# Pairs of neighbouring PSUM banks, the diagonal on GpSimd, and the last rows fetched by index, in a fused RWKV-6 and mixture-of-depths kernel

## The chip, the cores and the metric

The kernel runs on one core of a Trainium2 chip. A core has five engines that run side by side, each with its own queue of instructions, worked off in order: TensorE (PE; its weight loads are shown as PEld), VectorE (DVE), ScalarE (ACT), GpSimd (POOL) and SyncE (SP), which here issues most transfers. They wait for one another by semaphores. Data lies in SBUF, 128 rows of it, and matmuls write to PSUM, which has eight banks of 512 fp32 values a row. The metric is the device time of one execution, in microseconds (us).

## The reference, cut to what matters

```python
# attention: batch 4, heads 8, sequence 768, head size 48
for t in range(S):
    cur = np.einsum('bhd,bhe->bhde', u[None] * kt, vt)
    y[:, :, t] = np.einsum('bhd,bhde->bhe', rt, state + cur)
    state = wt[:, :, :, None] * state + np.einsum('bhd,bhe->bhde', kt, vt)
x = y.transpose(0, 2, 1, 3).reshape(B, S, H * D)          # 4 x 768 x 384

# mixture of depths: 128 of the 768 rows of each batch go through an expert
scores = np.einsum('bsd,d->bs', x, w_gate)
out = x.copy()
for b in range(B):
    top_idx = np.argpartition(-scores[b], capacity)[:capacity]
    xe = x[b, top_idx]
    ye = np.maximum(xe @ w1, 0.0) @ w2                    # 384 -> 1024 -> 384
    g = 1.0 / (1.0 + np.exp(-scores[b, top_idx]))
    out[b, top_idx] = x[b, top_idx] + g[:, None] * ye
```

A state that decays with w runs along the sequence. The term with u is each time step's own contribution: r times u times k, summed over the head's 48 values, times v of the same step. That number per head and time step is what the kernel calls "own", and it stands on the diagonal of the matrix of scores.

## The kernel before, in words

The sequence of each batch is cut into steps of 256 time steps (two chunks of 128), and the eight heads into two groups of four. A unit n is one step of one group of one batch: 4 batches x 3 steps x 2 groups = 24 units. `attention(P, n)` lists the work of a unit:

- SP loads w, k, r and v (line 257). The tiles have six buffers each, so a load waits until the unit six earlier is done with its buffer.
- POOL multiplies neighbouring rows of w (`w01`, L423), ACT takes the logarithm (`ln`, L427), PE sums it along the time with a triangular matrix (`U`, L432), DVE adds (`three`, L436), and ACT takes three exponentials of the result (`K1`, `K0`, `R`, L440 to L447). PE and ACT make the decay of a chunk (`D`, L457; `dec`, L462), and ACT applies it to the carried state (`begin`, L471).
- DVE scales k and r with the exponentials (`kr`, L479). PE transposes the result in two parts (`tr0`, `tr1`, L511), and ACT copies them out of PSUM (`cp0`, `cp1`, L520, tile krt).
- For the diagonal, POOL multiplies r by k and by u (`rk`, L488, and `ru`, L490), DVE sums over the head (`own`, L493), and ACT writes each sum on a diagonal of the score tile `sc` (`diag`, L501): eight small activations, `diag` (a 0/1 pattern of 128x64) times one number a row.
- PE makes the chunk's contribution to the state (`kv`, L537), DVE decays and adds it (`mid`, L549 and L554; `end`, L562).
- PE makes the scores (`S`, L609) and the first half of the product with the carried state (`rs1`, L578). DVE copies the scores that lie before the diagonal over the tile `sc` with a mask (`choose`, L626). PE then multiplies by v (`av`, L594) and adds the rest of the product with the state (L578 again).
- ACT copies the output out of PSUM (`x`, L641). DVE sums it with the gate's weights (`gate`, L649). After the second group of a step SP stores the rows (L664), and `compare` begins the ranking: PE spreads the scores (`ev`, L674), ACT copies them (`every`, L677), DVE counts which are larger (`cmp`, L680).

After six units a batch is complete and `mixture(P, b)` lists the rest. PE and DVE finish the rank (`columns`, L698; `rank`, L707), DVE marks for each of 128 places the row that has it (`pick`, L710), PE turns that into row numbers (`chosen`, L716; `idx`, L722). POOL fetches the rows from the output in HBM by index (`fetch`, L732), PE transposes them (`xt`, L744), ACT copies (`xec`, L754), and PE runs the two products of the expert (`p0` to `p7`, L788; `s0` to `s7`, L800) with ACT's relu in between (L794). DVE joins gate, product and row (`ye`, L805), and POOL scatters the rows back (`put`, L808). For the last batch (`held`) the rows' transpose is not taken from the fetched rows: PE gathers it from the rows of x that still lie in SBUF, by 18 fp32 products with `pick` (L747). There `pick` and the row numbers are fp32; elsewhere they are bf16. The fetch is made there too, for the gate and the sum at the end.

What sets the order is a written table. `Plan.add` only lists an operation with its engine, a planned duration, what it reads and writes, and which PSUM banks it opens or closes. Each operation gets a place `n + PHASE[name]` (for `mixture` n is the unit after the batch), and each engine does its operations in order of these places. The numbers only order the operations of one engine. `Plan.order` goes through the engines' queues with the planned durations, to settle the order of the program and which bank each PSUM tile gets. All PSUM is one tile, `psum`, of eight banks. `kv`, `S` and the output `Y` open two banks each, all other PSUM work one. Before the change any two free banks, those free for longest, made a pair (a, z), seen as `psum[:, a:z + 1:z - a, :]`. Operations marked `lock` are those of POOL and DVE that the planner keeps from running at the same time. SP, POOL's transfers and the waits follow from the same lists: an operation waits for those it depends on, and everything behind it in its engine's queue waits with it.

Of the kernel before, what the change touches and what calls it, by code (L numbers as in the profile page):

```python
# [18 lines left out]
L = 128  # L19
# [9 lines left out]
    "mid": -3.387, "cross": -3.695, "end": -3.208, "S": -2.042, "rs1": -2.003, "choose": -3.097,  # L29
# [3 lines left out]
    "won": 0.735, "columns": 2.189, "rank": 1.054, "pick": 1.358, "chosen": 3.464, "idx": 2.603,  # L33
    "fetch": 4.846, "rows": -40.331, "xt": 5.06, "xec": 6.795, "gates": 5.066, "gexp": 8.198,
# [3 lines left out]
    "s7": 14.354, "gate": -2.165, "krk": -0.95, "krr": -0.9, "c_table": -27.848,  # L38
    "c_strict": -29.361, "c_ident": -30.222, "c_iota": -32.474, "c_sums0": -28.494,
    "c_kr0": -65.518, "c_mask": -38.859, "c_sc0": -6.477, "c_sums1": -20.14, "c_kr1": -14.021,  # L40
    "c_sc1": -7.253, "c_sums2": -7.757, "c_kr2": -5.147, "c_sc2": -34.768, "c_ones": -41.327,
    "c_front": 0.4, "c_count": -37.113, "c_slots": -25.476,
# [13 lines left out]
class Plan:  # L56
# [37 lines left out]

    def order(self, banks):
# [15 lines left out]
        while len(out) < len(ops):  # L111
            best = None
            for e in line:
                if head[e] == len(line[e]):
                    continue
                n = line[e][head[e]]
                o = ops[n]
                count = sum(c for _, c in o["opens"])
                if any(seen[d] is None for d in o["deps"]) or count > len(free):
                    continue  # L120
                s = clock[e]
                if e == "PE" and o["tiles"] != tiles:
                    s += self.TURN[o["tiles"]]
                for d in o["deps"]:
                    s = max(s, ends[d] + self.AGAIN[e] if ops[d]["eng"] == e else seen[d])
                asked = s
                if o["lock"]:
                    s = max(s, port)
                if count:
                    s = max(s, sorted(free.values())[count - 1])  # L130
                if (best is None or s < best[0] - 1e-9 or s < best[0] + 1e-9 and o["lock"]
                        and ops[best[1]]["lock"] and asked < best[2]):
                    best = (s, n, asked)
            assert best is not None, "the order cannot be kept"
            s, n, _ = best
            o = ops[n]
            e = o["eng"]
            if e == "PE":
                tiles = o["tiles"]
            for name, c in o["opens"]:  # L140
                got = sorted(free, key=lambda i: (free[i], i))[:c]
                place[name] = tuple(sorted(got))
                for i in got:
                    free.pop(i)
            ends[n] = clock[e] = s + o["dur"]
            seen[n] = ends[n] + self.DELAY[e]
# [32 lines left out]
def kernel(  # L179
# [49 lines left out]
    def view(where):  # L229
        if len(where) == 1:  # L230
            return psum[:, where[0], :]
        a, z = where
        return psum[:, a:z + 1:z - a, :]
# [16 lines left out]
    xs = several(NT // 2, [L, 2, C], "x")  # L250
# [32 lines left out]
    pick32 = consts.tile([L, NT, L], FP32, name="pick32")  # L283
    ids32 = consts.tile([L, B, NT, 2], FP32, name="ids32")
# [19 lines left out]
    def constants(P):  # L304
# [81 lines left out]
        def _(_):  # L386
# [7 lines left out]
            nc.vector.tensor_copy(out=ids32, in_=ids)  # L394


    def attention(P, n):
# [7 lines left out]
        x = xs[step]  # L405
# [5 lines left out]
        X = f"x{step}"  # L411
# [61 lines left out]
        if not first:  # L473
            P.add("ACT", 0.22, lambda _: decayed(0, before, 0),
# [23 lines left out]
        def diagonal(_):  # L498
            for j in range(J):
                for i in (0, 1):  # L500
                    nc.scalar.mul(  # L501
                        ct[:, j % 2, j // 2, i, i, :], diag, ot[:, j % 2, j // 2, i:i + 1]
                    )
        P.add("ACT", 0.95, diagonal, reads=[OW, "mask"], writes=[SC], at=n, cls="diag")


# [180 lines left out]
    def mixture(P, b, held=False):  # L687

# [3 lines left out]

        pk, numbers = (pick32, ids32) if held else (pick, ids)

        def columns(ps):
# [15 lines left out]
            out=pk, in0=_free(slots, [0, NT], [1, L]), in1=rank.to_broadcast([L, NT, L]),  # L711
            op=ALU.is_equal), reads=["rank", "slots"], writes=["pick"], at=at, cls="pick", lock=True)

        def chosen(ps):
            for c in range(NT):
                nc.tensor.matmul(  # L716
                    ps[:, 0:2], pk[:, c, :], numbers[:, b, c, :],
                    start=(c == 0), stop=(c == NT - 1),
                )
        P.add("PE", 0.7 if held else 0.2, chosen, reads=["pick", "ids"], writes=[ID], at=at, cls="chosen",  # L720
# [19 lines left out]
        def turned(ps):  # L740
            for dc in range(NDC):
                at_dc = slice(dc * L, (dc + 1) * L)
                if not held:
                    nc.tensor.transpose(ps[:, at_dc], xe[z][:, at_dc], ident)  # L744
                    continue
                for c in range(NT):
                    nc.tensor.matmul(  # L747
                        ps[:, at_dc], xs[c // 2][:, c % 2, at_dc], pk[:, c, :],
                        start=(c == 0), stop=(c == NT - 1),
                    )  # L750
        P.add("PE", 2.1 if held else 0.35, turned, reads=["pick"] + [
            f"x{c}{g}" for c in range(NT // 2) for g in (0, 1)] if held else [f"xe{z}"], writes=[XT], at=at, cls="xt", opens=[(XT, 1)],
# [81 lines left out]
    for n in range(N):  # L834
        attention(P, n)
        if n % NU == NU - 1:
            mixture(P, n // NU, held=n == N - 1)
# [88 lines left out]
```

## Time and profile before

| | |
|---|---|
| median of the runs | 236.13 us (231.27 to 239.29, three runs) |
| the profiled execution | 236.0 us, of which the span from first to last instruction is 234.3 |
| mean granted TensorE clock in it | 0.943 |
| busy PE, PEld, DVE, ACT, POOL | 186.0, 158.9, 140.5, 143.2, 87.3 us |
| transfers | 29.44 MB, most of it in packets under 512 bytes |

Rows of instruction groups give a line, an engine, an operation, the tile written and the tiles read, sizes and a count; then the busy time and the mean duration of one in ns; then the idle time of the engine just before them and what ended it. Rows in order of time give the start, the duration, the instruction, and in brackets the idle time before it. Rows of waits give who waited for whom: us in total, times, longest. An fp32 matmul of the expert shows as two records. Matmuls overlap, and their ends are modelled, so PE's busy time is no measure of its best use.

### The profile page before, as it was taken

The numbers are of one execution on the slowest core, as the hardware profiler recorded it, in microseconds if no ns is written. First come the engines' busy times: TensorE is split into PE (matmuls) and PEld (weight loads), VectorE is DVE, ScalarE is ACT, GpSimd is POOL, SyncE is SP. The second block draws the span as 40 slices with busy tenths as digits, with TensorE's granted clock in tenths as the row PEclk, the third lists the DMA queues.
The fourth block names the chain that finished last, engine by engine and source line by source line (L and its number), as shares of the span: only waits on it lengthen the run. The fifth ranks groups of instructions, "written<-read, shape, count | busy, mean of one in ns | idle before, by whom it ended". The sixth has DMA issues, their size and how long they took to land.

```text
span 234.3 us, 10156 instructions
## 1 busy us (share of the span) xinstructions
PE 186.0 (79%) x4313; PEld 158.9 (68%) x4313; DVE 140.5 (60%) x400; ACT 143.2 (61%) x529; POOL 87.3 (37%) x99
## 2 busy tenths in 40 slices
PE   1868977696887697667787979796977999999960
PEld 0657766695777596665786966585966786979830
DVE  7747778687787858656768575659475346410110
ACT  3889889798998768688378475576365342110200
POOL 8876664355355554535315414307000110110110
PEclk9999999999999979799799799999799899999995
DMA  6999999897986948776244013202002103020101
GB/s 159 277 230 272 222 262 255 230 235 178 291 210 151 277 113 250 169 182 165 65 104 105 7 34 86 53 3 70 3 3 69 38 6 99 3 67 0 35 1 48
DMA packets 56853, 29.44 MB, mean 126 GB/s; under 512 B 51296, under 2 KB 55648, under 8 KB 56800
## 3 DMA queue, kind: packets, MB, share of 16 engines
q1 hardware_dynamic: 56288, 27.14, 44.7%
q0 software_dynamic: 512, 1.57, 2.4%
q8 instruction: 36, 0.59, 1.1%
q14 instruction: 17, 0.14, 0.2%
HBM read 23.20 MB, written 5.51 MB: 123 GB/s over the span
## 4 chain that ended last, share of the span: by engine, by line
PE 55%; ACT 16%; DVE 16%; issue 6%; POOL 2%; DMA 2%; SPq 0%; POOLq 0%; DVEq 0%; ACTq 0%
ACT sc L501 12%; PE psum L788 10%; PE psum L594 10%; DVE sc L626 9%; PE psum L511 9%; PE psum L800 8%; PE psum L537 3%; PE psum L609 3%; PE psum L578 3%; PE psum L432 3%; DMA u_bc<-in_u_dram 2%; ACT x L641 2%; PE psum L747 2%; PE psum L674 1%; DVE kr L479 1%
## 5 line engine op out<-in xcount | busy, mean ns | idle before, releaser
L488 POOL TENSOR_TENSOR rk<-kr_in 128x384 f32<-128x384 f32 x24 | 36.4, 1518 | 79.3 <-DVE own L493 75.9
L501 ACT ACTIVATE sc<-diag,own 128x64 f32<-128x64 f32 x192 | 48.5, 341 | 0.6 <-DVE own L493 0.6
L626 DVE COPY_PREDICATED sc<-mask,psum 128x1024 f32<-128x1024 uint32 x24 | 31.2, 1301 | 15.5 <-ACT sc L501 10.9
L511 PE MATMUL psum<-ident,kr 128*112 128x128 f32 x192 | 32.4, 314 | 9.3 <-DVE sc L626 6.8
L511 PEld LDWEIGHTS psum<-ident,kr 128*112 128x112 f32 x192 | 26.2, 154 | 12.3 <-DVE sc L626 7.9
L609 PE MATMUL psum<-krt 48*64 48x128 f32 x768 | 30.0, 274 | 5.0 <-ACT x L641 3.9
L520 ACT COPY krt<-psum 112x512 f32<-112x512 f32 x48 | 28.0, 584 | 8.4 <-PE psum L511 5.8
L594 PEld LDWEIGHTS psum<-v_in,sc 64*64 64x64 f32 x1536 | 25.8, 139 | 7.0 <-DVE sc L626 3.2
L594 PE MATMUL psum<-v_in,sc 64*64 64x48 f32 x1536 | 29.1, 224 | 1.9 <-DVE sc L626 1.6
L609 PEld LDWEIGHTS psum<-krt 48*64 48x64 f32 x768 | 23.0, 133 | 7.1 <-ACT x L641 5.3
L788 PE MATMUL psum<-xeT,w 128*128 128x128 f32 x192 | 27.1, 292 | 0.0
L788 PEld LDWEIGHTS psum<-xeT,w 128*128 128x128 f32 x192 | 25.6, 208 | 1.6 <-issue 0.6
L578 PE MATMUL psum<-st,krt 48*64 48x48 f32 x640 | 22.6, 219 | 4.9 <-issue 3.9
L432 PE MATMUL psum<-logs,strict 128*128 128x192 f32 x48 | 15.1, 402 | 13.5 <-DVE sc L626 7.9
L641 ACT COPY x<-psum 128x384 f32<-128x384 f32 x24 | 11.6, 482 | 21.4 <-PE psum L537 13.9
L490 POOL TENSOR_TENSOR rk<-rk,u_bc 128x384 f32<-128x384 f32 x24 | 23.9, 999 | 0.7 <-DMA u_bc<-in_u_dram 0.7
L800 PE MATMUL psum<-w,hid 128*128 128x384 f32 x64 | 23.8, 501 | 0.0
L578 PEld LDWEIGHTS psum<-st,krt 48*64 48x64 f32 x640 | 18.8, 134 | 7.1 <-issue 5.5
L479 DVE TENSOR_TENSOR kr<-kr_in,exps 128x768 f32<-128x768 f32 x24 | 23.4, 975 | 0.0
L808 POOL DMA_INDIRECT out_dram<-ye,idx x4 | 4.1, 1023 | 49.9 <-DVE ye L805 27.8
L554 DVE CUSTOM_DVE_ANT_0 st<-psum,st,dec 112x48 f32<-112x48 f32 x32 | 8.5, 267 | 21.3 <-ACT x L641 12.3
L432 PEld LDWEIGHTS psum<-logs,strict 128*128 128x128 f32 x48 | 8.5, 221 | 16.5 <-DVE sc L626 9.5
(93 smaller groups left out, 298.1 us busy)
## 6 DMA issues: line engine op xcount, KB each, us to landing
w_in<-in_w_dram SPq DMA_DIRECT2D x24, 192.0 KB, 4.4
kr_in<-in_k_dram SPq DMA_DIRECT2D x24, 192.0 KB, 4.4
kr_in<-in_r_dram SPq DMA_DIRECT2D x24, 192.0 KB, 4.4
v_in<-in_v_dram SPq DMA_DIRECT2D x24, 192.0 KB, 4.2
out_dram<-x SPq DMA_DIRECT2D x24, 192.0 KB, 3.5
w<-in_moe_w_dram SPq DMA_DIRECT2D x4, 768.0 KB, 5.9
u_bc<-in_u_dram SPq DMA_DIRECT2D x1, 192.0 KB, 5.0
wg_bc<-in_moe_w_gate_dram SPq DMA_DIRECT2D x1, 192.0 KB, 5.7
```

The lines of the kernel that those rows point to most:

```text
L432: P.add("PE", 0.33, lambda ps: nc.tensor.matmul(ps[:, 0:JD], strict, lt[:, 0], start=True, stop=True), reads=[LG, "strict"], writes=[U], a ...
L479: nc.vector.tensor_tensor(out=_free(kt, [DP, 2 * J], [2 * J * DP, 2], [1, D]), in0=krt_in.rearrange("p x j i d -> p (x j) i d"), in1=et.re ...
L488: P.add("POOL", 0.955, lambda _: nc.gpsimd.tensor_mul(rt, krt_in[:, 0], krt_in[:, 1]), reads=[KRI + "k", KRI + "r"], writes=[RK], at=n, cl ...
L501: nc.scalar.mul(ct[:, j % 2, j // 2, i, i, :], diag, ot[:, j % 2, j // 2, i:i + 1])
L511: nc.tensor.transpose(ps[0:CH, a * L:(a + 1) * L], kt[:, i, xx, 2 * m:2 * m + 2, :].rearrange("p j d -> p (j d)")[:, 0:CH], ident,)
L520: P.add("ACT", 0.48, lambda ps, i=i: nc.scalar.copy(out=_free(tt[0:CH, :, :, :, i], [L, 4 * M], [1, DP]), in_=_free(ps[0:CH], [DP, 4 * M], ...
L578: ins = nc.tensor.matmul(y[DP * i:DP * i + DP, c, j * D:j * D + D], tt[rows, 1, m, c, i, :], t0[rows, m, c, :], start=(i, c) not in fresh, ...
L594: nc.tensor.matmul(y[DP * to:DP * to + DP, c, j * D:j * D + D], ct[rows, jj, m, i, to, :], vt[rows, j, i, :], start=(to, c) not in fresh, ...
L609: nc.tensor.matmul(ps[DP * c:DP * c + DP, jj, (2 * m + i) * L:(2 * m + i + 1) * L], tt[rows, 0, m, c, i, :], tt[rows, 1, m, c].rearrange(" ...
L626: ins = nc.vector.copy_predicated(out=_free(ct, [4 * L, 2], [2 * L, M], [1, 2 * L]), mask=_free(mask, [0, 2], [0, M], [1, 2 * L]), data=_f ...
L788: nc.tensor.matmul(ps[:, q * L:(q + 1) * L], w1[:, dc, (f0 + q) * L:(f0 + q + 1) * L], xeT[z][:, dc, :], start=(dc == 0), stop=(dc == NDC ...
L800: nc.tensor.matmul(ps[:, 0:C], hid[:, fc, :], w2[:, fc, :], start=(fc == 0), stop=(fc == NFC - 1))
```

## The change

Five things change.

1. A pair of banks is now two neighbours, (0,1), (2,3), (4,5) or (6,7), and is seen without a stride. A single tile prefers a bank whose neighbour is taken, then the highest.
2. The diagonal is one product on GpSimd (`nc.gpsimd.tensor_tensor`, 512 elements a row, in the place of eight activations on ACT). It is marked `lock`.
3. `mixture` has no `held` form: the last batch's rows are transposed from the fetched rows like the others', `pick` and the row numbers are bf16 there too, and the 32-bit copies of both go.
4. The table PHASE is new for nearly every operation, so all engines' orders differ.
5. The planned duration of `begin` is 0.5 instead of 0.22, and that of `xt` 0.4 instead of 0.35. The buffer of x is indexed by `n // 2 % 3`, which is the same buffer as before, as a batch has three steps.

```diff
 PHASE = {
-    "lw": -16.341, "lk": -12.804, "lr": -12.572, "lv": -10.117, "w01": -7.91, "ln": -6.41,
-    "U": -6.825, "three": -8.09, "K1": -4.867, "K0": -4.314, "R": -4.127, "D": -3.874,
-    "dec": -2.2, "begin": -2.116, "kr": -5.531, "rk": -4.835, "ru": -2.379, "own": -3.561,
-    "diag": -0.472, "tr0": -3.309, "tr1": -2.784, "cp0": -1.67, "cp1": -1.11, "kv": -2.053,
-    "mid": -3.387, "cross": -3.695, "end": -3.208, "S": -2.042, "rs1": -2.003, "choose": -3.097,
-    "av": -1.056, "x": 0.443, "gate0": 1.002, "gate1": 1.829, "store0": -3.873, "store1": -4.089,
+    "lw": -19.956, "lk": -14.194, "lr": -13.707, "lv": -11.853, "w01": -9.001, "ln": -5.665,
+    "U": -6.784, "three": -7.195, "K1": -4.047, "K0": -4.043, "R": -3.291, "D": -3.858,
+    "dec": -1.201, "begin": -1.179, "kr": -4.644, "rk": -1.745, "ru": -1.545, "own": -2.747,
+    "diag": -0.997, "tr0": -3.414, "tr1": -2.548, "cp0": -0.483, "cp1": -0.099, "kv": -2.303,
+    "mid": -2.615, "cross": -3.695, "end": -2.573, "S": -2.224, "rs1": -2.183, "choose": -2.219,
+    "av": -1.234, "x": 1.68, "gate0": 1.002, "gate1": 1.829, "store0": -5.522, "store1": -6.249,
...
-    "fetch": 4.846, "rows": -40.331, "xt": 5.06, "xec": 6.795, "gates": 5.066, "gexp": 8.198,
-    "gates2": 8.47, "relu0": 9.181, "relu4": 11.338, "ye": 13.438, "put": 14.666, "p0": 6.223,
+    "fetch": 5.162, "rows": -5.835, "xt": 4.924, "xec": 7.896, "gates": 7.88, "gexp": 14.231,
+    "gates2": 12.739, "relu0": 9.834, "relu4": 12.566, "ye": 13.349, "put": 16.204, "p0": 5.83,
...
+    @staticmethod
+    def groups(free, count):
+
+        if count == 1:
+            return [(i,) for i in sorted(free)]
+        return [(i, i + 1) for i in sorted(free) if i % 2 == 0 and i + 1 in free]
...
-                    s = max(s, sorted(free.values())[count - 1])
+                    s = max(s, min(max(free[i] for i in g) for g in self.groups(free, count)))
...
-                got = sorted(free, key=lambda i: (free[i], i))[:c]
-                place[name] = tuple(sorted(got))
+                can = [g for g in self.groups(free, c) if max(free[i] for i in g) <= s + 1e-9]
+
+                got = max(can, key=lambda g: (g[0] ^ 1 not in free, g[0])) if c == 1 else can[0]
+                place[name] = got
...
-        return psum[:, a:z + 1:z - a, :]
+        return psum[:, a:z + 1, :]
...
         def diagonal(_):
-            for j in range(J):
-                for i in (0, 1):
-                    nc.scalar.mul(
-                        ct[:, j % 2, j // 2, i, i, :], diag, ot[:, j % 2, j // 2, i:i + 1]
-                    )
-        P.add("ACT", 0.95, diagonal, reads=[OW, "mask"], writes=[SC], at=n, cls="diag")
+            nc.gpsimd.tensor_tensor(
+                out=_free(ct, [2 * L, 2 * M], [L + DP, 2], [1, DP]),
+                in0=_free(diag, [0, 2 * M], [0, 2], [1, DP]),
+                in1=_free(ot, [2, 2 * M], [1, 2], [0, DP]), op=ALU.mult,
+            )
+        P.add("POOL", 1.0, diagonal, reads=[OW, "mask"], writes=[SC], at=n, cls="diag", lock=True)
...
         def turned(ps):
             for dc in range(NDC):
-                at_dc = slice(dc * L, (dc + 1) * L)
-                if not held:
-                    nc.tensor.transpose(ps[:, at_dc], xe[z][:, at_dc], ident)
-                    continue
-                for c in range(NT):
-                    nc.tensor.matmul(
-                        ps[:, at_dc], xs[c // 2][:, c % 2, at_dc], pk[:, c, :],
-                        start=(c == 0), stop=(c == NT - 1),
-                    )
+                nc.tensor.transpose(ps[:, dc * L:(dc + 1) * L], xe[z][:, dc * L:(dc + 1) * L], ident)
```

More of the change, by code (lines that the diff above doesn't have):

```diff
@@ L24 @@
 PHASE = {
[4 rows of a table removed]
-    "mid": -3.387, "cross": -3.695, "end": -3.208, "S": -2.042, "rs1": -2.003, "choose": -3.097,
[3 rows of a table removed]
-    "won": 0.735, "columns": 2.189, "rank": 1.054, "pick": 1.358, "chosen": 3.464, "idx": 2.603,
-    "fetch": 4.846, "rows": -40.331, "xt": 5.06, "xec": 6.795, "gates": 5.066, "gexp": 8.198,
[3 rows of a table removed]
[L38 to L42, printed above, removed]
[4 rows of a table added]
+    "mid": -2.615, "cross": -3.695, "end": -2.573, "S": -2.224, "rs1": -2.183, "choose": -2.219,
[3 rows of a table added]
+    "won": 1.507, "columns": 2.529, "rank": 1.903, "pick": 2.228, "chosen": 3.402, "idx": 2.825,
+    "fetch": 5.162, "rows": -5.835, "xt": 4.924, "xec": 7.896, "gates": 7.88, "gexp": 14.231,
[3 rows of a table added]
+    "s7": 11.534, "gate": -1.239, "krk": -0.95, "krr": -0.9, "c_table": -37.627,
+    "c_strict": -14.829, "c_ident": -2.405, "c_iota": -35.565, "c_sums0": -31.877,
+    "c_kr0": -35.325, "c_mask": -31.468, "c_sc0": -24.276, "c_sums1": -34.038, "c_kr1": -29.772,
+    "c_sc1": -25.745, "c_sums2": -53.736, "c_kr2": -7.291, "c_sc2": -26.658, "c_ones": -27.636,
+    "c_front": -8.276, "c_count": -10.913, "c_slots": -27.46,
 }
@@ L118, in order @@
                 count = sum(c for _, c in o["opens"])
-                if any(seen[d] is None for d in o["deps"]) or count > len(free):
+                if any(seen[d] is None for d in o["deps"]) or count and not self.groups(free, count):
                     continue
@@ L249 @@
     dec = several(3, [L, M, 2], "dec")
-    xs = several(NT // 2, [L, 2, C], "x")
+    xs = several(3, [L, 2, C], "x")
     half = consts.tile([L, 2, 2], FP32, name="half")
@@ L282 @@
     pick = consts.tile([L, NT, L], BF16, name="pick")
-    pick32 = consts.tile([L, NT, L], FP32, name="pick32")
-    ids32 = consts.tile([L, B, NT, 2], FP32, name="ids32")
     idx = several(2, [L, 1], "idx", UINT32)
@@ L393, in _ @@
             nc.vector.tensor_copy(out=ids[:, :, :, 1], in_=_free(low, [0, B], [0, NT]))
-            nc.vector.tensor_copy(out=ids32, in_=ids)
     def attention(P, n):
@@ L404, in attention @@
         t0, en, before = st0[n % 4], end[n % 4], end[(n - 2) % 4]
-        x = xs[step]
+        x = xs[n // 2 % 3]
         W, KRI, V = f"w_in{n % NB}", f"kr_in{n % NB}", f"v{n % NB}"
@@ L410, in attention @@
         T0, END = f"st0{n % 4}", f"end{n % 4}"
-        X = f"x{step}"
+        X = f"x{n // 2 % 3}"
         DEC = f"dec{n % 3}"
@@ L473, in attention @@
         if not first:
-            P.add("ACT", 0.22, lambda _: decayed(0, before, 0),
+            P.add("ACT", 0.5, lambda _: decayed(0, before, 0),
                   reads=[f"end{(n - 2) % 4}", DEC], writes=[T0 + "0"], at=n, cls="begin")
@@ L685, in compare, with mixture @@
             writes=[("ahead", b % 2, c), ("won", b % 2, c)], at=n, cls=f"cmp{z}", lock=True)
-    def mixture(P, b, held=False):
+    def mixture(P, b):
         z = b % 2
@@ L691, in mixture @@
         RA, ID, XT = ("ra", b), ("id", b), ("xt", b)
-        pk, numbers = (pick32, ids32) if held else (pick, ids)
         def columns(ps):
@@ L710, in mixture @@
         P.add("DVE", 0.87, lambda _: nc.vector.tensor_tensor(
-            out=pk, in0=_free(slots, [0, NT], [1, L]), in1=rank.to_broadcast([L, NT, L]),
+            out=pick, in0=_free(slots, [0, NT], [1, L]), in1=rank.to_broadcast([L, NT, L]),
             op=ALU.is_equal), reads=["rank", "slots"], writes=["pick"], at=at, cls="pick", lock=True)
@@ L716, in chosen @@
                 nc.tensor.matmul(
-                    ps[:, 0:2], pk[:, c, :], numbers[:, b, c, :],
-                    start=(c == 0), stop=(c == NT - 1),
+                    ps[:, 0:2], pick[:, c, :], ids[:, b, c, :], start=(c == 0), stop=(c == NT - 1)
                 )
-        P.add("PE", 0.7 if held else 0.2, chosen, reads=["pick", "ids"], writes=[ID], at=at, cls="chosen",
+        P.add("PE", 0.2, chosen, reads=["pick", "ids"], writes=[ID], at=at, cls="chosen",
               opens=[(ID, 1)], uses=ID)
@@ L741, in turned @@
             for dc in range(NDC):
-                at_dc = slice(dc * L, (dc + 1) * L)
-                if not held:
-                    nc.tensor.transpose(ps[:, at_dc], xe[z][:, at_dc], ident)
-                    continue
-                for c in range(NT):
-                    nc.tensor.matmul(
-                        ps[:, at_dc], xs[c // 2][:, c % 2, at_dc], pk[:, c, :],
-                        start=(c == 0), stop=(c == NT - 1),
-                    )
-        P.add("PE", 2.1 if held else 0.35, turned, reads=["pick"] + [
-            f"x{c}{g}" for c in range(NT // 2) for g in (0, 1)] if held else [f"xe{z}"], writes=[XT], at=at, cls="xt", opens=[(XT, 1)],
+                nc.tensor.transpose(ps[:, dc * L:(dc + 1) * L], xe[z][:, dc * L:(dc + 1) * L], ident)
+        P.add("PE", 0.4, turned, reads=[f"xe{z}"], writes=[XT], at=at, cls="xt", opens=[(XT, 1)],
               uses=XT)
@@ L836 @@
         if n % NU == NU - 1:
-            mixture(P, n // NU, held=n == N - 1)
+            mixture(P, n // NU)
     with tc.manual_schedule():
```

8 rows, old and new, of the table PHASE are left out of this document.

## The prediction

> **What bounds the kernel now.** I read the page's head and chain of waits, then busy time by stage, then the starts of one step per unit, then who waits for whom.
>
> ```profile
> span 234.3 us, 10156 instructions
> ...
> PE 186.0 (79%) x4313; PEld 158.9 (68%) x4313; DVE 140.5 (60%) x400; ACT 143.2 (61%) x529; POOL 87.3 (37%) x99
> ...
> ACT  3889889798998768688378475576365342110200
> ...
> ACT sc L501 12%; PE psum L788 10%; PE psum L594 10%; DVE sc L626 9%; PE psum L511 9%; PE psum L800 8%; PE psum L537 3%; PE psum L609 3%; PE psum L578 3%; PE psum L432 3%; DMA u_bc<-in_u_dram 2%; ACT x L641 2%; PE psum L747 2%; PE psum L674 1%; DVE kr L479 1%
> ```
>
> No engine is full over the span, and yet the diagonal on ACT (L501) is the largest line of the chain. So the kernel is bound by hand-overs; where, the stages tell. Columns: window, length, then busy us of PE, weight loads, DVE, ACT, POOL; granted clock, DMA share, GB/s.
>
> ```profile
> 16.00:110.00 94.00, 73.90 (x2331) 65.41 (x2323) 69.72 (x190) 79.92 (x308) 48.49 (x48) 0.96 0.83 216
> 110.00:193.00 83.00, 69.92 (x1698) 60.69 (x1698) 50.97 (x147) 47.80 (x173) 21.76 (x19) 0.92 0.19 49
> 193.00:227.00 34.00, 33.24 (x228) 26.21 (x221) 9.42 (x34) 4.57 (x11) 3.07 (x4) 1.00 0.13 36
> 95.00:99.00 4.00, 3.49 (x47) 3.06 (x51) 2.88 (x6) 2.23 (x10) 1.16 (x2) 0.57 0.87 196
> ```
>
> Each unit has one predicated copy (L626). Of its 24 starts the first, the fifteenth and the last are these:
>
> ```profile
> 17.96 1.33 DVE L626 COPY_PREDICATED sc<-mask,psum 128x1024 f32<-128x1024 uint32 x1 [0.69 <-ACT sc L501]
> ...
> 111.14 1.29 DVE L626 COPY_PREDICATED sc<-mask,psum 128x1024 f32<-128x1024 uint32 x1 [1.85 <-PE psum L432]
> ...
> 188.86 1.31 DVE L626 COPY_PREDICATED sc<-mask,psum 128x1024 f32<-128x1024 uint32 x1 [0.74 <-ACT sc L501]
> ```
>
> Stage one, 14 intervals: (111.14-17.96)/14 = 6.66 us a unit. Stage two, where the expert's matmuls lie between the units, 9 intervals: (188.86-111.14)/9 = 8.64 us. The first window holds 14 of these copies, the second 10, so busy time per unit is ACT 79.92/14 = 5.71, PE 5.28, DVE 4.98, POOL 3.46 in stage one (ACT leads, at 86% of 6.66) and PE 6.99, DVE 5.10, ACT 4.78 in stage two (PE leads, at 81% of 8.64). The tail is PE alone, 33.24 of 34.
>
> ```profile
> POOL rk L488 <- DVE own L493: 75.9, 19, 6.5
> ...
> ACT x L641 <- PE psum L537: 13.9, 13, 2.2
> DVE st L554 <- ACT x L641: 12.3, 6, 3.6
> DVE sc L626 <- ACT sc L501: 10.9, 18, 1.0
> ...
> PE psum L432 <- DVE sc L626: 7.9, 5, 1.9
> ...
> PE psum L511 <- DVE sc L626: 6.8, 4, 2.1
> ...
> PE psum L609 <- ACT x L641: 3.9, 8, 0.6
> ```
>
> Columns: us in total, times, longest. The copy waits for the diagonal in 18 of 24 units. The lines with x are odd: L609 (scores) and L554 (state) share no data with the copy x, and x does not need L537 (kv). Two neighbouring units in order of time:
>
> ```profile
> 118.35 0.48 ACT L641 COPY x<-psum 128x384 f32<-128x384 f32 x1 [1.30 <-PE psum L537]
> 118.86 0.27 DVE L554 CUSTOM_DVE_ANT_0 st<-psum,st,dec 112x48 f32<-112x48 f32 x1 [3.19 <-ACT x L641]
> ...
> 118.88 1.10 PE L609 MATMUL psum<-krt 48*64 48x128 f32 x32 [0.60 <-ACT x L641]
> ...
> 124.64 0.48 ACT L641 COPY x<-psum 128x384 f32<-128x384 f32 x1 [0.23 <-PE psum L578]
> ...
> 125.66 0.41 DVE L649 CUSTOM_DVE_ANT_0 junk<-psum,wg_bc,half 128x192 f32<-128x192 f32 x1
> ```
>
> In the first, x waits for kv, and both L554 and L609 start within 0.05 us of its end (118.83); in the second, x starts on L578, the last of its own inputs. The code is the same, only the banks differ. My reading, an inference: a pair seen with a stride counts as all banks from its lower to its upper one, so pairs that cross order one another.
>
> **The change, part by part.**
>
> *The diagonal.*
>
> ```profile
> L501 ACT ACTIVATE sc<-diag,own 128x64 f32<-128x64 f32 x192 | 48.5, 341 | 0.6 <-DVE own L493 0.6
> ...
> L490 POOL TENSOR_TENSOR rk<-rk,u_bc 128x384 f32<-128x384 f32 x24 | 23.9, 999 | 0.7 <-DMA u_bc<-in_u_dram 0.7
> L479 DVE TENSOR_TENSOR kr<-kr_in,exps 128x768 f32<-128x768 f32 x24 | 23.4, 975 | 0.0
> ```
>
> ```profile
> L423 POOL TENSOR_TENSOR w_in<-w_in 128x192 f32<-128x192 f32 x24 | 15.7, 653 | 0.5 <-DMA w_in<-in_w_dram 0.4
> ...
> L493 DVE TENSOR_REDUCE own<-rk 128x8 f32<-128x384 f32 x24 | 13.1, 547 | 2.6 <-POOL rk L490 2.6
> ```
>
> ```profile
> L488 POOL TENSOR_TENSOR rk<-kr_in x24: 997/1644/1651, 8.0 to 158.8; 128x384 f32<-128x384 f32 x24
> ```
>
> It takes 48.5/24 = 2.02 us a unit from ACT: 5.71 becomes 3.69 in stage one and 2.76 in stage two. POOL gets one product of 512 elements a row. Two products give the price: (999-653)/192 = 1.80 ns an element, so 999+128x1.80 = 1.23 us (estimate). Bounds: 1.0 (the 384-element product) and 1.88: L488 has a minimum of 0.997 and a median of 1.644, 0.65 us more when it starts just behind own, where DVE does kr (L479); the diagonal starts there too. I take 1.23, the unblocked rows, for POOL's load, and 1.88 for the loop below. POOL rises to 3.46+1.23 = 4.69 us a unit, under PE's 5.28. It is idle today mainly because rk waits for own (75.9 us).
>
> The new order puts diagonal n ahead of rk n+1. Behind the diagonal's wait for own stand rk, ru and the fetches; for ru waits own, for own all later DVE work. That loop is own 0.55, diagonal 1.88, rk 1.00, ru 1.00, and four hand-overs of about 0.1 (an estimate from the 0.05 us above, doubled): 4.8 us, 5.5 if rk is blocked too (w01, 0.65, lies in the wait for own). Both are under 6.66.
>
> So PE leads both stages, with 5.28 and 6.99 us, and waits remain: the copy after the gates of the unit before, and U and the transposes after the copy. Today's leaders reach 86% and 81%; I take 88% for PE, a choice a little above both, because two causes of waits go (the diagonal, and x's odd ones). Stage one: 5.28/0.88 = 6.00, 14 x 0.66 = -9.2 us. Stage two: 6.99/0.88 = 7.94, 9 x 0.70 = -6.3 us. Bounds: at 98% as in the tail, 5.39 and 7.13, -17.8 and -13.6; at no better use than now, 0. The rows by themselves agree in size: 10.9 for the diagonal plus 3.9 for the scores is 14.8 against my 15.5.
>
> *The pairs.* Neighbours don't cross, which frees x, L554 and L609 (inside the above). Against it: two free banks that are no neighbours don't serve. Bounds: 0, and the PSUM rival below.
>
> *The clock.*
>
> ```profile
> 95.51 1.01 PE L432 MATMUL psum<-logs,strict 128*128 128x192 f32 x2 [1.93 <-DVE sc L626]
> ```
>
> After PE's wait of 1.93 us the clock averaged 0.57 in the four us from 95, and L432 needed 1.01. Over stages one and two the mean clock costs 0.04x94+0.08x83 = 10.4 us of full-speed work. With less waiting I expect 40% back, -4 us (bounds: 0 and -10.4, choice nearer to 0 since waits remain). The Trainium skill (TensorE: Matmul & The Clock Gate, What's actually happening) says the clock halves after at least one idle window of about 3.4 us. The trace disagrees: it halved around a wait of 1.93. By the page's rule this term would be 0 and the total 217.
>
> *The last batch.*
>
> ```profile
> 139.05 0.29 PE L716 MATMUL psum<-ids,pick 128*128 128x2 bf16 x6
> ```
>
> ```profile
> 196.51 0.49 PE L744 MATMUL psum<-ident,xe 128*128 128x128 f32 x3
> ...
> 203.51 1.40 PE L716 MATMUL psum<-ids,pick 128*128 128x2 f32 x12
> ...
> 206.63 0.22 DVE L722 TENSOR_SCALAR idx<-psum 128x1 uint32<-128x1 f32 x1 [2.81 <-DMA out_dram<-ye,idx]
> ...
> 209.42 4.18 PE L747 MATMUL psum<-pick,x 128*128 128x128 f32 x36
> 210.29 0.56 DVE L762 CUSTOM_DVE_ANT_0 junk<-xe,wg_bc 128x384 f32<-128x384 f32 x1 [3.44 <-DMA xe<-out_dram,idx]
> ```
>
> ```profile
> 115.85 0.67 PE psum L788 x6
> ...
> 150.80 1.29 PE psum L800 x4
> ```
>
> PE saves 4.18-0.49 and 1.40-0.29, 4.8 us, in a stage that is PE alone. New is that the transposes wait for the fetched rows, 210.29-206.63 = 3.66 us after the index starts. The new order's phases put five products of L800 (two records each, 0.65 us) and one of L788 (0.67) between choice and transposes: 3.9 us of cover. I take 1 us of wait (0 to 2; uncovered 3.7): -3.8 us. PE's remaining products queue behind it, and the last scatter waits for them.
>
> *Loads and start.*
>
> ```profile
> v_in<-in_v_dram SPq DMA_DIRECT2D x24, 192.0 KB, 4.2
> ```
>
> ```profile
> 3.49 0.51 SPq L257 DMA_DIRECT2D kr_in<-in_r_dram  x1
> ```
>
> In SP's queue v of unit n now stands behind w of n+8 (before: n+6), whose buffer is free once Ln of n+2 is done. ACT does that beside the first krt copy of n-3, so v leaves some three units, 18 us, ahead of its kv and lands in 4.2: 0; without that cover it would cost those 4.2 a unit. The stores keep their place ahead of k of n+9, but behind a w that waits about a unit longer; only fetches wait for them, and the last store has no load ahead of it: 0. At the start the order is new: seven w01 go ahead of the first rk, and r of unit 0 moves from sixth to ninth load. The u load stays fourteenth in SP's queue, v of unit 0 moves one place back. I take 0, bounds -2 and +2, from four places at 0.51 us, one load's issue. The indices of xs, the dropped 32-bit copies and the planned 0.5 for "begin" issue nothing new: 0.
>
> Sum against the profiled execution, 236.0 us (span 234.3): -9.2-6.3-4-3.8 = -23.3, 212.7, forecast **213**. The median of the runs, 236.1, is the same.
>
> **The rivals.**
>
> *Direct waits only, 222.* The odd waits of x are true ones and the copy is then held by the gates. Gone are 10.9 and 3.8: 236-14.7 = 221.3, with a little either way 218 to 229. For it: ACT is only 4.78 of 8.64 in stage two. Against: the two units above. 18%.
>
> *PSUM, no change.* Eight banks must hold kv, scores and two outputs, all pairs, beside single ones for U, D and the transposes. If a single one splits a pair, kv waits for the copy in every unit. PE's waits on that release are 7.9+6.8 = 14.7 us in nine cases, 1.6 each; in all 24 that is 39, 24 more, and the gain of 23.3 is gone: 236 to 237. The point is 23.3/24 = 0.97 us a unit. 11%.
>
> *PSUM, slower.* The same place, but the scores' pair also waits, for the gates that free the older output, 0.82 us (two of 0.41, L649 above), 24 times, +20: 256. It is slower by 2% from 1.17 us of extra wait a unit. For it: the nine cases. Against: singles are put where the neighbour is taken. 7%.
>
> *GpSimd's loop, slower.* It passes 6.66 if the diagonal, own and the products block one another: if the diagonal needs over 3.7 us, or if DVE's kr is held behind it each time. The Trainium skill (SBUF — State Buffer, Who interferes with whom) has it that a DVE instruction with two SBUF inputs and a GpSimd one that reads SBUF lock each other out, whole instructions at a time. L488's 1.64 against 0.997 agrees; that kr loses is against the 975 ns mean of L479, which hardly moves beside 72 POOL products. A kr held by 1.23 in each of 24 units costs 30 us: 213+30 = 243. 4%.
>
> **How the numbers follow.** Forecast 60%, 202 to 220: 202 is 236 less the larger bounds of stages and tail (17.8, 13.6 and about 3). Direct waits 18%, PSUM 11% and 7%, GpSimd 4%. The range 202 to 231 holds forecast and direct waits, less a small part of the forecast below 202 and plus a little of the PSUM case with partial waits: 8 in 10. A difference of 2% (4.7 us) is about what can be told from no change; faster 60+18 = 78%, within 11%, slower 7+4 = 11%.
>
> **What would show it.** The diagonal at POOL near 1.2 to 1.9 us; ACT's busy time near 95; no start of L609 or L554 on x; units of about 6.0 and 7.9 us; a clock row with fewer dips; a tail without L747 and at most 2 us of PE wait for the fetched rows. I am wrong if PE's waits on the predicated copy rise above 39 us, if rk and the diagonal fill POOL, or if PE's use stays at 81%.

## The result, and the profile after

The changed kernel takes 209.07 us (median of 4 runs, 204.08 to 212.63) against 235.02 us before (4 runs, 231.27 to 239.29). The ratio is 0.882, 95% interval 0.853 to 0.910; ratios here and below are made of undisturbed runs alone, and so need not equal the quotient of the medians, and the profiles of two runs below (any two banks again, the last version) are of disturbed executions. The profiled execution took 206.1 us with a span of 204.0, which is 30.3 less than before. Against the 236.0 of the profile before that is a ratio of 0.873, so the stages below add up to a little more than 0.882 says.

The page of the changed kernel, its head, two rows of the span in 40 slices, and the chain that ended last. Line numbers differ from those before by up to seven (L505 diagonal, L615 scores, L632 predicated copy, L647 x, L600 av, L543 kv, L584 product with the state, L517 transposes of k and r, L781 and L793 the expert's products, L438 `U`, L463 `D`). The first line is the clock row of the page before, for comparison; all others are of the page after.

```profile
PEclk9999999999999979799799799999799899999995
...
span 204.0 us, 10003 instructions
...
PE 172.0 (84%) x4274; PEld 148.3 (73%) x4274; DVE 140.5 (69%) x399; ACT 102.5 (50%) x337; POOL 112.3 (55%) x123
...
ACT  3787467854687675448826852465345123111200
...
PEclk9999979997899999999999999999999999999995
...
PE 75%; issue 9%; DVE 6%; ACT 4%; POOL 3%; POOLq 0%; DVEq 0%
PE psum L600 11%; PE psum L615 11%; PE psum L793 10%; PE psum L781 10%; PE psum L517 9%; PE psum L584 6%; PE psum L543 6%; PE psum L438 5%; PE psum L463 3%; PE psum L680 3%; DVE sc L632 1%; PE psum L701 1%; DVE ahead L686 1%; ACT logs L433 1%; DVE sums L442 1%
```

The diagonal has left the chain, the predicated copy has nearly done so (9% to 1%), and three quarters of the chain are PE. Busy time by stage (columns as before: window, length, busy PE, weight loads, DVE, ACT, POOL, then clock, DMA share, GB/s). The windows are cut at the first, the fifteenth and the last predicated copy:

```profile
18.58:105.58 87.00, 73.32 (x2298) 64.87 (x2297) 68.70 (x187) 55.27 (x186) 60.86 (x59) 0.96 0.82 218
105.58:165.69 60.11, 58.16 (x1604) 52.20 (x1604) 47.71 (x139) 29.52 (x93) 31.29 (x27) 1.00 0.28 74
165.69:204.00 38.31, 30.82 (x277) 23.82 (x276) 11.88 (x42) 5.69 (x15) 5.28 (x5) 0.93 0.15 44
```

And the kernel before, cut at its own copies:

```profile
17.96:111.14 93.18, 73.12 (x2299) 64.61 (x2297) 68.56 (x187) 79.10 (x304) 46.96 (x47) 0.96 0.83 216
111.14:188.86 77.72, 65.30 (x1593) 56.81 (x1594) 48.69 (x140) 45.80 (x167) 20.73 (x18) 0.91 0.19 48
188.86:234.30 45.44, 36.92 (x322) 29.50 (x320) 11.83 (x42) 5.43 (x13) 5.10 (x5) 0.93 0.12 33
```

| | before | after | difference | forecast |
|---|---|---|---|---|
| to the first copy | 17.96 | 18.58 | +0.6 | 0 |
| stage one (a unit) | 93.2 (6.66) | 87.0 (6.21) | -6.2 | -9.2 (6.00) |
| stage two (a unit) | 77.7 (8.64) | 60.1 (6.68) | -17.6 | -6.3 (7.94), and a share of the clock's -4 |
| from the last copy on | 45.4 | 38.3 | -7.1 | -3.8 |

Stage two is where the time went. PE is busy in 58.16 of its 60.11 us, 97%, at full clock; before it was busy in 65.30 of 77.72, 84%, at a mean clock of 0.91. Who waited (us in total, times, longest):

```profile
POOL sc L505 <- DVE own L499: 44.9, 19, 4.0
...
ACT x L647 <- PE psum L584: 21.5, 16, 3.2
...
PE psum L615 <- issue: 8.4, 7, 2.2
...
DVE sc L632 <- PE psum L584: 5.2, 5, 2.3
...
PE psum L584 <- issue: 2.5, 3, 1.7
...
PE psum L600 <- issue: 1.9, 3, 1.6
```

x now waits for L584, its own last input, and no longer for kv. Neither the scores nor the state wait for x. The copy no longer waits for the diagonal. What has grown are pauses of PE for nothing that the profile shows ("issue"): 8.4+2.5+1.9 = 12.8 us, against 5.8 before; 11.6 of the 12.8 lie in stage one.

### The profile page after: what moved, and what is told of

Read it like the earlier page. It is cut to its first block, busy times and chain, and to the rows that moved or that the text cites. A ratio compares the mean times of both kernels' runs of the same rounds, so it can differ in the third digit from the quotient of the medians.

```text
span 204.0 us, 10003 instructions
## 1 busy us (share of the span) xinstructions
PE 172.0 (84%) x4274; PEld 148.3 (73%) x4274; DVE 140.5 (69%) x399; ACT 102.5 (50%) x337; POOL 112.3 (55%) x123
## 4 chain that ended last, share of the span: by engine, by line
PE 75%; issue 9%; DVE 6%; ACT 4%; POOL 3%; POOLq 0%; DVEq 0%
PE psum L600 11%; PE psum L615 11%; PE psum L793 10%; PE psum L781 10%; PE psum L517 9%; PE psum L584 6%; PE psum L543 6%; PE psum L438 5%; PE psum L463 3%; PE psum L680 3%; DVE sc L632 1%; PE psum L701 1%; DVE ahead L686 1%; ACT logs L433 1%; DVE sums L442 1%
## 5 line engine op out<-in xcount | busy, mean ns | idle before, releaser
L505 POOL TENSOR_TENSOR sc<-diag,own 128x512 f32<-128x512 f32 x24 | 37.4, 1557 | 52.3 <-DVE own L499 44.9
L615 PE MATMUL psum<-krt 48*64 48x128 f32 x768 | 31.3, 275 | 8.4 <-issue 8.4
L632 DVE COPY_PREDICATED sc<-mask,psum 128x1024 f32<-128x1024 uint32 x24 | 31.5, 1312 | 8.3 <-PE psum L584 5.2
L600 PE MATMUL psum<-v_in,sc 64*64 64x48 f32 x1536 | 30.2, 219 | 2.2 <-issue 1.9
L615 PEld LDWEIGHTS psum<-krt 48*64 48x64 f32 x768 | 24.0, 133 | 9.4 <-issue 9.4
L600 PEld LDWEIGHTS psum<-v_in,sc 64*64 64x64 f32 x1536 | 26.7, 133 | 2.7 <-issue 2.6
L517 PE MATMUL psum<-ident,kr 128*112 128x128 f32 x192 | 28.4, 290 | 0.0
L584 PE MATMUL psum<-st,krt 48*64 48x48 f32 x640 | 24.3, 221 | 3.8 <-issue 2.5
L781 PE MATMUL psum<-xeT,w 128*128 128x128 f32 x192 | 25.8, 278 | 0.0
L517 PEld LDWEIGHTS psum<-ident,kr 128*112 128x112 f32 x192 | 24.1, 144 | 2.2 <-issue 0.6
L781 PEld LDWEIGHTS psum<-xeT,w 128*128 128x128 f32 x192 | 23.9, 191 | 2.4
L584 PEld LDWEIGHTS psum<-st,krt 48*64 48x64 f32 x640 | 20.9, 137 | 5.6 <-issue 4.3
L494 POOL TENSOR_TENSOR rk<-kr_in 128x384 f32<-128x384 f32 x24 | 24.7, 1028 | 0.1
L793 PE MATMUL psum<-w,hid 128*128 128x384 f32 x64 | 24.3, 493 | 0.0
L647 ACT COPY x<-psum 128x384 f32<-128x384 f32 x24 | 11.5, 480 | 21.9 <-PE psum L584 21.5
L438 PE MATMUL psum<-logs,strict 128*128 128x192 f32 x48 | 15.3, 407 | 8.1 <-ACT logs L433 6.1
L683 ACT COPY every<-psum 128x128 f32<-128x128 f32 x24 | 6.4, 267 | 25.7 <-PE psum L680 25.7
L655 DVE CUSTOM_DVE_ANT_0 junk<-psum,wg_bc,half 128x192 f32<-128x192 f32 x24 | 10.0, 416 | 13.0 <-ACT x L647 11.2
L686 DVE SCALAR_TENSOR_TENSOR ahead<-every,score,front 128x128 bf16<-128x128 f32 (+5 forms) x24 | 16.9, 710 | 1.2 <-ACT every L683 1.2
```

What stands on the lines that cost most here:

```text
L438: P.add("PE", 0.33, lambda ps: nc.tensor.matmul(ps[:, 0:JD], strict, lt[:, 0], start=True, stop=True), reads=[LG, "strict"], writes=[U], a ...
L494: P.add("POOL", 0.955, lambda _: nc.gpsimd.tensor_mul(rt, krt_in[:, 0], krt_in[:, 1]), reads=[KRI + "k", KRI + "r"], writes=[RK], at=n, cl ...
L505: nc.gpsimd.tensor_tensor(out=_free(ct, [2 * L, 2 * M], [L + DP, 2], [1, DP]), in0=_free(diag, [0, 2 * M], [0, 2], [1, DP]), in1=_free(ot, ...
L517: nc.tensor.transpose(ps[0:CH, a * L:(a + 1) * L], kt[:, i, xx, 2 * m:2 * m + 2, :].rearrange("p j d -> p (j d)")[:, 0:CH], ident,)
L584: ins = nc.tensor.matmul(y[DP * i:DP * i + DP, c, j * D:j * D + D], tt[rows, 1, m, c, i, :], t0[rows, m, c, :], start=(i, c) not in fresh, ...
L600: nc.tensor.matmul(y[DP * to:DP * to + DP, c, j * D:j * D + D], ct[rows, jj, m, i, to, :], vt[rows, j, i, :], start=(to, c) not in fresh, ...
```

## The experiments

Ratios are to the kernel before, run on the same chip in the same series. The changed kernel itself ran in none of these series; its 0.882 (0.853 to 0.910) is of the runs above. Each experiment has one profile.

### One part alone

Neighbouring pairs alone:

```diff
...
+        return [(i, i + 1) for i in sorted(free) if i % 2 == 0 and i + 1 in free]
...
-        return psum[:, a:z + 1:z - a, :]
+        return psum[:, a:z + 1, :]
```

> The kernel before with neighbouring pairs alone (order, diagonal on ACT and last batch as before). Theory (crossing pairs order one another): the waits of the scores (L609) and of the state (L554, L549) on the copy x are gone, x waits for L578 and not for kv, and the time falls by 4 to 12 us (ratio 0.95 to 0.98). Rival (the stride is harmless, neighbours are only a restriction): those waits stay in number and length, ratio 0.99 to 1.03.

Measured: 208.5 us, ratio 0.903 (0.892 to 0.914), a larger gain than the theory's 0.95 to 0.98. Waits of this kernel (L650 is x, L587 the product with the state, L635 the copy, L563 the state), and its stages, cut as above:

```profile
ACT x L650 <- PE psum L587: 12.4, 13, 2.8
...
DVE sc L635 <- ACT sc L510: 7.4, 12, 1.2
...
DVE st L563 <- ACT x L650: 2.3, 3, 1.8
```

```profile
17.36:99.94 82.58, 72.31 (x2294) 62.77 (x2293) 67.93 (x188) 77.52 (x302) 47.17 (x47) 0.98 0.90 241
99.94:161.91 61.97, 58.82 (x1605) 51.67 (x1604) 48.95 (x140) 45.78 (x169) 20.75 (x18) 1.00 0.25 62
161.91:205.80 43.89, 36.08 (x314) 28.70 (x312) 11.73 (x42) 5.43 (x13) 5.09 (x5) 0.94 0.12 35
```

x waits for its own input, the scores never for x. The state's wait on x was 18.7 us before, the 12.3 of L554 and the 6.4 of L549:

```profile
DVE st L549 <- ACT x L641: 6.4, 3, 3.4
```

It has gone to 2.3. Stage one is shorter than the changed kernel's (82.6 against 87.0 us) and stage two 1.9 us longer (62.0 against 60.1), with the diagonal still on ACT and the old order; the clock of stage two is 1.00. The end is 43.9 us, nearly as long as before (45.4).

The diagonal on GpSimd alone:

```diff
-    "diag": -0.472,
+    "diag": -2.0,
...
-                    nc.scalar.mul(ct[:, j % 2, j // 2, i, i, :], diag, ot[:, j % 2, j // 2, i:i + 1])
+            nc.gpsimd.tensor_tensor(out=..., in0=diag..., in1=ot..., op=ALU.mult)
```

> The kernel before with the diagonal as one product on GpSimd alone, placed between ru of its unit and rk three units on. Theory (the ACT queue holds the copy): the 10.9 us of the predicated copy's wait for the diagonal go, some of ACT's other delays too, ratio 0.94 to 0.97. Rival (the gates hold the copy in any case, or GpSimd's loop takes ACT's place): ratio 0.98 to 1.02, and the copy waits for the gates or for GpSimd instead.

Measured: 233.2 us, ratio 1.011 (1.003 to 1.019). The rival holds in its number; its reason is another. The waits of this kernel, with the lines of the kernel before:

```profile
DVE st L554 <- ACT x L641: 17.3, 10, 3.0
...
ACT x L641 <- PE psum L609: 12.5, 7, 3.2
...
ACT x L641 <- PE psum L537: 10.1, 7, 3.0
...
PE psum L609 <- ACT x L641: 2.9, 6, 0.6
```

The copy's 10.9 us of waiting for the diagonal are gone, and x now waits 12.5 us for the scores (L609), which it does not read, and still 10.1 for kv. So x is still held behind kv and the scores with the diagonal off ACT; that this is what holds the unit is argued from these waits, and the run of the pairs alone fits it.

The fetch alone, with `mixture` as in the change:

> The kernel before with the last batch fetched by index like the others, alone. Theory: PE's tail loses 4.8 us and gains some 1.2 us of wait for the fetched rows, so 3 to 4 us less, ratio about 0.985. Rival (the fetch is exposed): the wait is 4 us or more, ratio 1.00.

Measured: 232.9 us, ratio 1.012 (0.996 to 1.028): no difference that can be told, and the theory's 0.985 lies outside the interval. Only within its profile is the stretch from the last copy to the end shorter, as the theory had it: 228.9-186.5 = 42.4 us against 45.4, so 3.0 us less. PE's wait for the rows is in the trace:

```profile
207.56 0.55 PE L735 MATMUL psum<-ident,xe 128*128 128x128 f32 x3 [1.40 <-DMA xe<-out_dram,idx]
```

The new order alone (any two banks, the diagonal on ACT at "diag": 0.70, the gathered last batch):

> The new order alone: pairs of any two banks seen with a stride, the diagonal on ACT (placed in ACT's queue behind x of the unit before) and the gathered last batch. Theory (the parts carry the gain, the order only fits them): ratio 0.96 to 1.02. Rival (the order carries most of the gain): ratio 0.92 or less.

Measured: 251.2 us, 246.2 to 251.4, with 230.8 to 240.2 for the kernel before beside it; no ratio is on record. Neither had it: in this form, with the diagonal in ACT's queue, the order alone makes the kernel slower.

### One part undone

Any two banks again, in the changed kernel:

> The changed kernel with pairs of any two banks again, seen with a stride. Theory (crossing pairs order one another): waits of the scores or the state on x come back, ratio to the kernel before 0.91 to 0.95 (some 7 to 14 us slower than the changed kernel's 0.88). Rival (the stride is harmless): 0.87 to 0.89, perhaps better, since any two banks serve.

Measured: 227.3 us, ratio 0.971 (0.958 to 0.983). The theory's waits come back, here of x on the scores (L606) and of the product with the state (L575) on x, and the price is above what it said:

```profile
ACT x L638 <- PE psum L606: 24.6, 10, 5.7
...
PE psum L575 <- ACT x L638: 4.5, 7, 0.9
```

The diagonal on ACT again, behind x of the unit before ("diag": 0.70):

> The changed kernel with the diagonal on ACT again, behind x of the unit before. Theory (ACT's 2.02 us a unit stand between x and the predicated copy): 24 units lose 0.4 to 1 us each, ratio to the kernel before 0.92 to 0.97. Rival (PE sets the pace and the diagonal is hidden): 0.88 to 0.90.

Measured: 214.0 us, ratio 0.921 (0.911 to 0.931). The copy waits for it again, in 19 of 24 units:

```profile
DVE sc L632 <- ACT sc L507: 15.6, 19, 1.0
```

So with neighbouring pairs the diagonal's place does matter, about 9 us in this order (0.921 against 0.882, whose interval is wide). That is one place in ACT's queue; the run is slower than the pairs alone (0.903), where the old order has the diagonal on ACT too.

The gathered last batch again:

> The changed kernel with the last batch gathered by fp32 products again. Theory: PE's tail grows by 4.8 us, ratio to the kernel before about 0.90. Rival (the fetch cost as much as it saved): 0.88.

Measured: 213.0 us, 207.1 to 214.4; no ratio is on record. The stretch from the last copy on is 205.4-162.0 = 43.4 us against 38.3, 5.1 us more, which fits the theory; the total doesn't tell.

The old order's table with all three parts ("diag": -2.0 on GpSimd):

> All three parts, but the old order's table (the diagonal on GpSimd between ru of its unit and rk three units on). Theory (the parts carry the gain): ratio to the kernel before 0.90 to 0.93. Rival (the order carries most): 0.96 or more.

Measured: 203.7 us, ratio 0.875 (0.864 to 0.885). It can't be told from the changed kernel (the intervals overlap), so no gain of the new order is shown. Against the pairs alone, in the same order, the diagonal and the fetch bring 0.903 to 0.875; by the profiles, cut at the copies, stage one goes from 82.6 to 82.3 us, stage two from 62.0 to 59.5 and the end from 43.9 to 40.3.

### Is it the span of a pair?

Fixed pairs as in the change, on the kernel before, but banks i and i+4:

```diff
-        return [(i, i + 1) for i in sorted(free) if i % 2 == 0 and i + 1 in free]
+        return [(i, i + 4) for i in sorted(free) if i < 4 and i + 4 in free]
-        return psum[:, a:z + 1, :]
+        return psum[:, a:z + 1:z - a, :]
```

> The kernel before with fixed pairs as in the change, but with banks i and i+4 as partners, seen with a stride of four banks; the same freedom as neighbours, and every pair's span crosses every other's. Theory (a strided pair is ordered as its whole span): the waits on x come back, more of them than before the change, ratio 1.00 or above. Rival (fixed partners and their packing gave the gain, not the span): 0.90, as with neighbours.

Measured: 243.4 us, ratio 1.046 (1.036 to 1.057). The same freedom as neighbours, and 0.903 has become 1.046. L546 is kv, L618 the scores:

```profile
ACT x L650 <- PE psum L546: 22.5, 19, 2.4
...
DVE st L563 <- ACT x L650: 14.2, 9, 2.9
...
PE psum L618 <- ACT x L650: 10.1, 20, 0.6
```

x waits for kv in 19 units and the scores wait for x in 20; before the change it was 13 and 8. The banks of each unit, as the kernel's own `Plan.order` gives them, say the same unit by unit. In the kernel before, 23 times an output is followed by the next unit's kv and scores, and never do they share a bank. In 17 of the 23 the span of the output's pair overlaps that of kv, and all 13 waits of x for kv are among these 17; in 17 it overlaps that of the scores, and all 8 waits of the scores for x are among those. In the prediction's two units the output at 118.35 has banks (0,6) and kv (3,7); at 124.64 it is (1,3) and (4,6), both seen with a stride, and x does not wait for kv. So it is not the stride as such.

Together this settles it: pairs whose spans overlap are ordered one behind the other, and neither packing nor fixed partners made the gain. Whether the program's bookkeeping sets the waits or the chip does these runs don't separate (the profile infers who released whom from semaphore events); that they are waits on instructions sharing no bank and no data they do show.

### GpSimd's slack, and the pauses

The diagonal's product issued twice, in the changed kernel:

> The changed kernel with the diagonal's product issued twice in a row on GpSimd (the same values written twice), 24 more products of 1.0 to 1.6 us. Theory (GpSimd has slack: 44.9 us of waiting for own before the diagonal): ratio to the kernel before 0.88 to 0.90. Rival (GpSimd's loop is at the bound in stage one): the whole product is paid in stage one, 14 x 1.3 us = 18 us, ratio 0.95 or more.

Measured: 206.0 us, ratio 0.886 (0.879 to 0.892), against 0.882. The second product is paid from GpSimd's waiting for own, which falls from 44.9 to 24.0 us; the copy waits a little for it (behind the edit, lines are one higher in this run and the next):

```profile
POOL sc L506 <- DVE own L499: 24.0, 22, 2.7
...
DVE sc L633 <- POOL sc L506: 5.8, 12, 0.8
```

The loads of k, r and v only for the first six units:

```diff
+        if n < NB:
             P.add("SP", 0.56, lambda _: load(k, krt_in[:, 0], n), ...)
```

> The changed kernel without the loads of k, r and v from the seventh unit on (those units compute with data of earlier ones, so the output differs), 54 of 96 unit loads. Theory (PE's pauses for nothing shown are its instructions arriving late beside the loads): the pauses before L615, L600 and L584 fall from 12.8 us to under 4, stage one to 5.8 us a unit or less, the time by 5 us or more. Rival (the pauses have another cause): they stay above 9 us.

Measured: 197.2 us, ratio 0.849 (0.841 to 0.858). These are two runs. The row of DMA use in 40 slices, and the pauses (L616 scores, L585 product with the state; av, now L601, has none):

```profile
DMA  6999972334732223649230120220300314111001
```

```profile
PE psum L616 <- issue: 2.5, 1, 2.5
PE psum L585 <- issue: 1.3, 2, 1.0
...
PE psum L544 <- issue: 0.5, 1, 0.5
```

The pauses on the three lines fall from 12.8 to 3.8 us, and stage one from 6.21 to (98.73-18.29)/14 = 5.75 us a unit, as the theory had it. But with all the loads in place the run with the product issued twice has 6.5 us of pauses, half the changed kernel's, and its stage one is as long as the changed kernel's all the same:

```profile
PE psum L616 <- issue: 3.3, 2, 2.7
PE psum L601 <- issue: 1.8, 3, 1.0
...
PE psum L585 <- issue: 1.4, 1, 1.4
```

```profile
18.59:105.93 87.34, 75.49 (x2299) 66.09 (x2298) 70.20 (x187) 55.22 (x186) 77.04 (x72) 0.94 0.79 209
```

The pairs alone have 5.6 us of pauses with the DMA engines at 0.90 in stage one. The changed kernel with the gathered last batch, whose units are the same, has a stage one of (101.58-17.94)/14 = 5.97 us. So the pauses differ from trace to trace by two thirds of what this run takes away, and the length of stage one does not follow them. That leaving out the loads makes the kernel faster is shown (0.849 against 0.886 in the same series); that the pauses come with the loads is not, nor that they are instructions arriving late: they fall inside runs of like matmuls, and their cause stays open.

### A version from the experiments

All three parts with the old order, and w01 ahead of the diagonal on GpSimd ("w01": -8.1, before -7.91):

> Neighbouring pairs, the diagonal on GpSimd and the fetch with the old order's table, and w01 moved one place on GpSimd, ahead of the diagonal, so that it runs while own is under way (with the old place ACT's logarithm waited 27 us in total for w01). Theory: that wait falls to under 10 us, ratio 0.86 to 0.875. Rival (the logarithm has slack): 0.875 to 0.885, as without the move.

Measured: 204.0 us, ratio 0.870 (0.861 to 0.879). ACT's wait for w01, without the move and with it:

```profile
ACT logs L433 <- POOL w_in L429: 27.0, 20, 2.9
```

```profile
ACT logs L433 <- POOL w_in L429: 3.2, 3, 2.2
```

The wait went, but the time can't be told from that without the move (0.875, 0.864 to 0.885). Most of the wait came back further on in ACT's queue, at the decay of a chunk (`dec`, L468, which waits for PE's `D`); again without the move and with it:

```profile
ACT dec L468 <- PE psum L463: 9.4, 9, 3.4
```

```profile
ACT dec L468 <- PE psum L463: 34.1, 20, 4.5
```

So ACT waited elsewhere, which fits the rival's slack, though the ratio lies in the theory's range; which of the two is right isn't shown. The version beats the kernel before; it can't be told from the changed kernel.

## Why the prediction was right or wrong

The time was right: 213 forecast, 209.07 measured, 206.1 against 212.7 for the profiled execution; faster by 12%. The reasons were right in kind and wrong in weight. That the total lay so near is in part luck: by the two profiles stage one gave 3.0 us less than its term, and stage two with the clock (17.6 against 6.3 and at most 4) and the tail (7.1 against 3.8) gave more.

- **The step that failed** is the sentence "10.9 for the diagonal plus 3.9 for the scores is 14.8 against my 15.5". It gave the diagonal the larger part and the odd waits of x the smaller. The pairs alone gave a ratio of 0.903, about four fifths of the gain to 0.882, and the diagonal alone 1.011. I priced the odd waits by the one line where PE waits (L609, 3.9 us) and left out that x and the state run late too, 13.9 and 18.7 us, and stand ahead of the diagonal and of the copy in ACT's and DVE's queues. That it is by this way that PE lost its time is argued from the order; what the pairs are worth is measured. A direct wait is no price either: in the run of the diagonal alone its 10.9 us went, and x waited 12.5 us for the scores instead.
- **The inference from the stride** held. The banks (i, i+4) made the waits nearly regular, and unit by unit they fall only where spans overlap.
- **88% of PE** as the use in both stages was the mis-sized term. Stage two reached 97%, stage one 73.32 of 87.00, 84%. Why stage one fell short stays open: PE's pauses there are 11.6 us, but with 5.5 of them, in the run with the product issued twice, it is as long, and the same units took 5.97 us instead of 6.21 in the run with the gathered last batch. The 81% that the prediction read for stage two set ten units of a window against nine intervals; cut at the copies, PE's use before was 65.30 of 77.72, 84%.
- **The clock** was sized too low. In stage two the mean went from 0.91 to 1.00, and PE's busy time from 65.30 to 58.16, about 7 us; I had 4 for both stages. Stage one stayed at 0.96. The Trainium skill (TensorE: Matmul & The Clock Gate, What's actually happening) asks for an idle window of about 3.4 us; by that rule nothing would have come here, and the trace disagrees again. PE's longest wait in stage two was 1.64 us before the change.
- **The diagonal's price** was 1.04 us at the least and 1.62 in the middle, in the bounds of 1.0 to 1.88, and DVE's kr hardly lost (981 ns a piece, 975 before):

```profile
L505 POOL TENSOR_TENSOR sc<-diag,own x24: 1043/1623/1689, 15.8 to 163.0; 128x512 f32<-128x512 f32 x24
```

```profile
L485 DVE TENSOR_TENSOR kr<-kr_in,exps 128x768 f32<-128x768 f32 x24 | 23.5, 981 | 0.2 <-DMA kr_in<-in_r_dram 0.2
```

  That it runs behind kr and waits agrees with the Trainium skill (SBUF — State Buffer, Who interferes with whom). Once the diagonal started first, and then it was kr that took 1.75 us instead of 0.95:

```profile
15.84 1.04 POOL L505 TENSOR_TENSOR sc<-diag,own 128x512 f32<-128x512 f32 x1
15.94 1.75 DVE L485 TENSOR_TENSOR kr<-kr_in,exps 128x768 f32<-128x768 f32 x1 [0.19 <-DMA kr_in<-in_r_dram]
```

  ACT's busy time fell to 102.5 and not to 95: its rows by group overlap (before, they add up to about 180 us where 143.2 are busy), so a row can't be taken from the total as it stands.
- **GpSimd's loop** as a rival fell: a second product was free. **The PSUM rivals** fell: no wait on the copy grew to their size, and PE's 14.7 us of them are gone. **Direct waits only, 222,** fell with the odd waits being real costs.
- **The tail** lost 7.1 us, not 3.8. The fetched rows were there in time. The transposes start right behind a run of products that began at 181.65:

```profile
180.43 0.22 DVE L724 TENSOR_SCALAR idx<-psum 128x1 uint32<-128x1 f32 x1 [0.87 <-PE psum L719]
...
181.65 2.75 PE L793 MATMUL psum<-w,hid 128*128 128x384 f32 x8
...
184.23 0.49 PE L744 MATMUL psum<-ident,xe 128*128 128x128 f32 x3
```

  So the cover of 3.9 us held, and the 1 us of wait I charged was none. PE's busy time there fell by 36.92-30.82 = 6.1, of which 4.8 are the dropped fp32 products (35.60 in the run that gathers again). The rest is in part work that the order had done earlier: with the old order and the same parts PE is busy 32.66 us of a stretch of 40.3.
- **The order** I treated as something that fits the parts. No gain of it is shown: alone it lost, and the old one with the same parts can't be told from it.

## What to carry to other kernels

A wait between two instructions that share no data is worth more study than a long one between two that do: look at how their operands lie (here the view of a pair of banks), and count everything that runs late behind it, not only the engine you care for. A direct wait in the profile bounds what its removal gives from neither side: the diagonal's 10.9 us gave nothing alone, and the scores' 3.9 us stood for far more. Try each part alone and each undone, for here one part of four carried most of the gain. Before a pause or a stage's length is put down to a cause, look at other traces of the same code: here they differed by half the effect and more.

## What the runs showed of the hardware that I had not expected

- PE stops for up to 2.2 us inside runs of matmuls, without a wait that the profile shows: 11.6 us in stage one of the changed kernel, 5.5 with the diagonal's product issued twice. The cause is open.
- TensorE's clock recovers as a whole with waits of under 2 us gone. Before the change it fell to 0.5 six times between 81 and 184 us, each time for about 3.4 us and near a wait of PE of 1.3 to 1.9 us; four of the six lay in stage two. With those waits gone stage two ran at 1.00 instead of 0.91, with the pairs alone as with the whole change. Not every such wait does it: in the changed kernel the clock stayed at 1.00 around waits of 1.58 and 2.21 us at 90 and 105 us.
- A GpSimd product of 512 elements a row with two broadcast inputs ran in 1.04 us in the 3 of 24 cases in which it did not start behind kr, hardly more than the 1.00 of a plain one with 384.
